# A 47-point Fourier stage moved from one 94x96 weight to four 47x64 weights in the quarters of the array

## The chip, the cores and the metric

The kernel runs on one core of one Trainium2 chip. The metric is the time of one execution on the device in microseconds (us); of several executions the median is taken. Below, PE is the matrix engine (TensorE), PEld its weight loads, ACT the ScalarE, DVE the VectorE, POOL the GpSimd engine, and SP the engine that issues most of the DMAs.

## What is computed

The reference has two parts, one behind the other. The first is a filter over the sequence, done in frequency space; the second is a two-layer network with a PReLU between its layers.

```python
X = np.fft.rfft(x, axis=1)                 # x: 8 batches, 3008 positions, 256 channels
Y = X * (filt_r + 1j * filt_i)[None]       # 1505 frequencies
y = np.fft.irfft(Y, n=3008, axis=1)
h = y.reshape(24064, 256) @ w_in           # 256 -> 2048
g = np.maximum(h, 0) + alpha * np.minimum(h, 0)
out = g @ w_out                            # 2048 -> 256
```

## The kernel before, in words

3008 is 47 times 64, so the transform of one batch is made in two stages. Stage a takes, for each of the 64 values of the position modulo 64 (called s) and for each of the 256 channels, a 47-point transform; only 24 of its 47 frequencies are needed, and their real and imaginary parts make 48 rows. Stage b makes the 64-point transforms with the twiddle factors in the weights, then the filter is applied, and stages c and d go back the same way. The result lies in `yT`, from which the network reads blocks of 512 positions.

The two parts run interleaved. The network has 47 blocks, each of 16 steps, so there are 752 steps, a little over 1 us each. In every step PE makes, in this order: the pieces of the transform that the plan puts at this step (`plan`, filled by `put`), the first layer of one slice of 128 hidden units (`up`, L616, two matmuls of 512 columns into `hps`), and a share of the second layer of an earlier block (L667, L689). The plan is fixed: the table `PLACES` holds, for each of batches 1 to 7, the step of every piece, and the same loops add the DMAs. Batch 0 has its own code (class `First`) and runs before the network starts. Engines take their instructions in the order in which the code issues them.

The pieces touched by the change are those of stage a of batches 1 to 7:

- `load_x` (L197) brings 8 values of s for each half (h = 0 is s below 32, h = 1 the rest) of one batch into a tile `xs`. Half 0 lies on partitions 0 to 46, half 1 on 47 to 93, with 8 x 256 values in each partition. Four such chunks c make a batch, with two DMAs on POOL's queue each (L201).
- `piece_a` (L237) multiplies the 94x96 weight `wf1_s`, which has the 47x48 matrix twice on its diagonal, with 512 columns of `xs` (L245), into one PSUM bank, and copies 96x512 values from there to `asb` on ACT (`on_act`, L324). 16 pieces make a batch, four a chunk.
- `save_a` (L249) writes the 96 partitions of `asb` to `a_dram` with one DMA from SP's queue (L250), once per chunk. When all four are written, `turn_a` (L252) reads them back in another order into `at` (L257), which stage b multiplies (`piece_b`, L261, matmuls at L265, copied by ACT at L269).

All pieces of stages a to d take their PSUM bank from `bank()` (L218): two pools `psF` of one bank each, used in turn. Whoever takes a bank waits until the copy out of its last user is done; so a user waits for the user two before it. The first layer has two tiles `hps` of its own, and ACT copies these too (L632).

In the setup, `turn_i` (L487) makes matmuls with weights of 64 columns, whose results go to PSUM partitions 0 to 63 and 64 to 127 in turn; line L502 has one matmul with 16 rows. Everything else uses the array as one tile of 128x128.

Of the kernel before, what the change touches and what calls it, by code (L numbers as in the profile page):

```python
# [10 lines left out]
FP16 = mybir.dt.float16  # L11
# [3 lines left out]
N1 = 47  # L15
N2 = 64
NK1 = 24
D = 256
# [60 lines left out]
def _build_consts():  # L79

    s1 = np.arange(N1)
    s2 = np.arange(N2)
    k1 = np.arange(NK1)
    p = np.arange(64)
    k2 = np.where(p < 32, p, 95 - p)
    g = np.where(p < 32, 1.0, -1.0)  # L90

    a1 = 2 * np.pi * np.outer(s1, k1) / N1
    wf1 = np.zeros((2 * N1, 96))
    wi3 = np.zeros((96, 2 * N1))
    scale = np.where(k1 == 0, 1.0, 2.0) / NFFT
    for h in range(2):
        r = slice(h * N1, h * N1 + N1)
        wf1[r, h * 48 : h * 48 + NK1] = np.cos(a1)
        wf1[r, h * 48 + NK1 : h * 48 + 48] = -np.sin(a1)
        wi3[h * NK1 : h * NK1 + NK1, r] = (np.cos(a1) * scale).T  # L100
        wi3[48 + h * NK1 : 48 + h * NK1 + NK1, r] = (-np.sin(a1) * scale).T

    kk = k1[:, None] + 47 * k2[None, :]
    ang = 2 * np.pi * s2[:, None, None] * kk[None, :, :] / NFFT
    c, s = np.cos(ang), np.sin(ang)
    twf = np.empty((128, NK1, 128))
    twf[:64, :, 64:], twf[64:, :, 64:] = c, s
    twf[:64, :, :64], twf[64:, :, :64] = -s * g, c * g
    return wf1, wi3, twf
# [3 lines left out]
def kernel(  # L113
# [9 lines left out]
):  # L123
    nc = tc.nc
    wf1_np, wi3_np, twf_np = _build_consts()
    wf1_d = nc.inline_tensor(wf1_np.astype(np.float16), name="c_wf1")
    wi3_np = wi3_np.reshape(4, NK1, 2 * N1).transpose(1, 0, 2).reshape(96, 2 * N1)
    wi3_d = nc.inline_tensor(wi3_np.astype(np.float16), name="c_wi3")
    wiz_np = np.zeros((3, 32, 4, 4, 2 * N1))
# [17 lines left out]
    konst = ctx.enter_context(tc.tile_pool(name="konst", bufs=1))  # L147
    p_x = ctx.enter_context(tc.tile_pool(name="p_x", bufs=4))
    p_fft = ctx.enter_context(tc.tile_pool(name="p_fft", bufs=1))
    p_as = ctx.enter_context(tc.tile_pool(name="p_as", bufs=2))  # L150
# [6 lines left out]
    a_dram = dram.tile([NB, 96, NH, D], FP16, name="a_dram")  # L157
# [1 line left out]
    ctx.enter_context(tc.manual_schedule())  # L159


    wf1_s = konst.tile([2 * N1, 96], FP16, name="wf1_s")
    wi3_s = konst.tile([96, 2 * N1], FP16, name="wi3_s")
    twf_s = konst.tile([128, NK1, 128], FP16, name="twf_s")
    twi_s = konst.tile([128, NK1, 128], FP16, name="twi_s")
# [18 lines left out]
    id16, wfx_s = idx_s[:, 0:128], idx_s[0 : 2 * N1, 128:224]  # L184
# [8 lines left out]
    def xrow(b, h, c):  # L193
        return bass.AP(tensor=x.tensor, offset=x.offset + (b * NFFT + NH * h + 8 * c) * D,
                       ap=[[N2 * D, N1], [1, 8 * D]])

    def load_x(b, c, halves=(0, 1)):  # L197
        if 0 in halves:
            xc[(b, c)] = p_x.tile([2 * N1, 8 * D], FP16, name="xs")
        for h in halves:  # L200
            nc.gpsimd.dma_start(out=xc[(b, c)][h * N1 : h * N1 + N1], in_=xrow(b, h, c))  # L201

    def load_filt(dst, pbase, src, ka, kb):
        n = kb - ka
# [13 lines left out]
    def bank(wide=False):  # L218
        if wide:
            return psH.tile([128, 2, 512], FP32, name="hps")[:, 0]  # L220
        turns[0] += 1
        return psF[turns[0] % 2].tile([128, 512], FP32, name="psF")
# [8 lines left out]
    class Fft:  # L231
# [2 lines left out]
            self.base = (b % 2) * NFFT  # L234
            self.uw, self.zt, self.asb = {}, {}, {}

        def piece_a(self, i, evict, wide=False):  # L237
            if i == 0:
                self.at = p_fft.tile([128, NK1, D], FP16, name="at")
            if i % 4 == 0:  # L240
                self.asb[i // 4] = p_as.tile([96, 8, D], FP16, name="asb")
            xs = xc[(self.b, i // 4)]
            ps = bank(wide)
            o = (i % 4) * 512
            nc.tensor.matmul(ps[0:96], wf1_s, xs[:, o : o + 512], start=True, stop=True)  # L245
            u = 2 * (i % 4)
            evict(self.asb[i // 4][:, u : u + 2].rearrange("p a d -> p (a d)"), ps[0:96])

        def save_a(self, c):  # L249
            nc.sync.dma_start(out=a_dram[self.b, :, 8 * c : 8 * c + 8], in_=self.asb[c])  # L250

        def turn_a(self, eng, ka=0, kb=NK1):  # L252
            for h in range(2):
# [78 lines left out]
    class First(Fft):  # L332
# [8 lines left out]
        def piece_a(self, i, evict, ps):  # L341
            c, sh, f = i // 4, (i // 2) % 2, i % 2
            for u in range(4):
                o = (4 * sh + u) * D + 128 * f
                nc.tensor.matmul(ps[:, 96 * u : 96 * u + 96], xc[(0, c)][:, o : o + 128], wfx_s,
                                 start=True, stop=True)
            s0 = 8 * c + 4 * sh
            evict(self.am.rearrange("p (f m s) -> p f m s", f=2, s=NH)[:, f, :, s0 : s0 + 4],
                  ps[:, 0:384].rearrange("p (s m) -> p m s", s=4))
# [78 lines left out]
    xc = {}  # L428
# [12 lines left out]
    for c in range(4):  # L441
        load_x(0, c)
# [120 lines left out]
    for c in range(4):  # L563
        load_x(1, c)
        if c == 0:
            load_w(1)
    for q in range(2):
        nc.gpsimd.dma_start(
            out=wout_s[:, 8 * q : 8 * q + 8],
            in_=moe_w_out[1024 * q : 1024 * q + 1024].rearrange("(j p) d -> p j d", p=128))  # L570
# [175 lines left out]
    def put(step, fn, *args):  # L746
        plan.setdefault(step, []).append((fn, args))
# [17 lines left out]
    for b in range(1, NB):  # L765
        p = 94 * (b - 1)
        f = Fft(b)
        steps_a, steps_b, steps_c, steps_d = PLACES[b - 1]
        for i in range(16):
            put(p + steps_a[i], f.piece_a, i, on_act)  # L770
            if i % 4 == 3:
                put(p + steps_a[i] + (b > 2), f.save_a, i // 4)
        if b + 1 < NB:
            for c in range(4):
                if b < 3:
                    put(LOADS[b - 1][c], load_x, b + 1, c)
                else:
                    for h in range(2):
                        put(p + LOADS[b - 1][2 * c + h], load_x, b + 1, c, (h,))
        quarters, later = (4, 1) if b < 3 else (1, 4)  # L780
        w = NK1 // quarters
        for q in range(quarters):
            put(p + steps_a[15] + (7 if b == 4 else later), f.turn_a, nc.sync, w * q, w * q + w)
        for kp in range(12):
            put(p + steps_b[kp], f.piece_b, kp)
            put(p + steps_c[kp], f.piece_c, kp, on_act)
            if kp % 3 == 2:
                put(p + steps_c[kp] + 1, f.turn_c, kp // 3)
        for i in range(16):
            put(p + steps_d[i], f.piece_d, i, on_act)  # L790
        put(p + steps_d[3] + 2, f.load_z, 3)
# [91 lines left out]
```

## Time and profile before

| what | us |
|---|---|
| median of 3 timed runs | 764.0 (763.15 to 765.53) |
| the profiled execution | 761.9 |
| its span, first to last instruction | 760.1 |
| PE busy in the span | 743.8 (98%) |
| DVE busy | 694.1 (91%) |
| ACT busy | 673.8 (89%) |
| stage a of batches 1 to 7: matmuls at L245 | 112 instructions, 35.7 to 549.6 |

The profile is one execution, recorded instruction by instruction. A row of a group names line, engine, operation, output and input tile, partitions x elements, and the count; then the busy time in us, the mean of one in ns, and the time for which the engine stood idle just ahead of these instructions, with what ended that. A row of the timeline begins with a start in us from the span's start and a length; "x7" says that seven instructions follow each other there, and the length reaches from the first one's start to the last one's end. The lengths of matmuls hold the passage through the array, so that consecutive matmuls overlap in the record: what a matmul costs PE is the distance from its start to the next one's.

### The profile page before, as it was taken

The page shows a single profiled execution, that of the slowest core. Times are in us where ns is not written, and L with a number is a line of the kernel's source. Part 1 is how long each engine was busy: PE and PEld are TensorE (multiplying, and loading weights), DVE is VectorE, ACT ScalarE, POOL GpSimd, SP SyncE. Part 2 cuts the span into 40 slices and gives each one's busy share as a digit, 9 for nine tenths or more (in the row PEclk, how much of TensorE's full clock was granted, in tenths as well). Part 3 has the DMA queues.
Part 4 walks back from the last instruction along what each step waited for, and adds up shares of the span by engine and source line. Part 5 has one row for each costly group of instructions (what it writes and reads, how often), then busy time and mean ns, then how long its engine had stood idle before and what let it go on. Part 6 is the DMA issues. An engine that isn't in the chain of part 4 may idle for free.

```text
span 760.1 us, 19854 instructions
## 1 busy us (share of the span) xinstructions
PE 743.8 (98%) x7812; PEld 539.9 (71%) x7812; DVE 694.1 (91%) x1298; ACT 673.8 (89%) x1083; POOL 163.8 (22%) x236
## 2 busy tenths in 40 slices
PE   6999999999999999999999999999999999999998
PEld 5756666776787777777778777777777777777766
DVE  5787887998999998899999999999998997999994
ACT  6898999999999988999899998999989898888873
POOL 8631421232022210232022211221100221010100
PEclk9999999999999999999999999999999999999999
DMA  9995888877965596766876659865486355522122
GB/s 160 196 236 152 148 182 214 174 149 170 211 150 114 120 192 160 148 121 140 189 161 143 136 117 197 187 141 113 106 185 135 77 105 113 138 63 66 43 65 62
DMA packets 100790, 107.97 MB, mean 142 GB/s; under 512 B 10568, under 2 KB 81496, under 8 KB 100696
## 3 DMA queue, kind: packets, MB, share of 16 engines
q1 hardware_dynamic: 80136, 70.05, 36.0%
q0 software_dynamic: 20416, 36.58, 29.8%
q8 instruction: 61, 1.00, 0.6%
q14 instruction: 33, 0.27, 0.1%
q10 hardware_dynamic: 144, 0.07, 0.0%
HBM read 55.41 MB, written 46.66 MB: 134 GB/s over the span
## 4 chain that ended last, share of the span: by engine, by line
PE 88%; DMA 5%; ACT 3%; POOL 2%; issue 1%; DVE 1%; DVEq 0%; POOLq 0%; ACTq 0%
PE hps L616 40%; PE op L689 30%; PE op L667 7%; PE psF L245 3%; PE psF L317 3%; PE psF L265 2%; PE psF L292 2%; DMA uw_s<-uw_s 2%; ACT gtb L632 2%; DMA xs<-in_x_dram 1%; DMA win_s<-in_moe_w_in_dram 1%; DMA filt<-in_filt_r_dram 1%; PE op L721 1%; ACT v L324 1%; POOL xs L201 1%
## 5 line engine op out<-in xcount | busy, mean ns | idle before, releaser
L616 PE MATMUL hps<-yT,win_s 128*128 128x512 f16 (+3 forms) x1600 | 447.4, 366 | 0.4 <-POOL win_s L575 0.4
L632 ACT ACTIVATE gtb<-hps 128x1024 f16<-128x1024 f32 x376 | 385.9, 1028 | 50.4 <-PE hps L616 47.5
L689 PEld LDWEIGHTS <-gtb 128*128 128x128 f16 x3040 | 206.0, 98 | 99.5 <-issue 0.3
L638 DVE TENSOR_SCALAR m_s<-gtb,alm_s 128x512 f16<-128x512 f16 x705 | 213.9, 347 | 38.4 <-ACT gtb L632 36.7
L819 DVE TENSOR_TENSOR gtb<-gtb,m_s 128x2048 f16<-128x2048 f16 x188 | 228.8, 1217 | 5.7 <-ACT m_s L636 3.2
L689 PE MATMUL op<-wout_s,gtb 128*128 128x128 f16 x1824 | 153.3, 219 | 0.0
L616 PEld LDWEIGHTS <-win_s 128*128 128x128 f16 x1600 | 135.4, 98 | 24.8 <-issue 2.9
L281 POOL DMA_DIRECT2D uw_s<-uw_s x84 | 72.3, 1003 | 330.0 <-DVE uw_s L278 205.7
L689 PEld LDWEIGHTS <-ss 128*128 128x128 f16 x1216 | 83.1, 98 | 37.4
L689 PE MATMUL op<-tw_s,gtb 128*128 128x128 f16 x1216 | 105.0, 219 | 0.0
L689 PE MATMUL op<-tw_s,ss 128*128 128x128 f16 x1216 | 103.4, 219 | 0.0
L667 PE MATMUL op<-wout_s,gtb 128*128 128x256 f16 x512 | 76.9, 273 | 0.3 <-DVE osb L592 0.3
L654 POOL DMA_DIRECT2D gtb<-gtb x28 | 28.5, 1017 | 208.0 <-ACT gtb L632 139.5
L667 PEld LDWEIGHTS <-gtb 128*128 128x128 f16 x512 | 49.9, 98 | 31.3
L324 ACT ACTIVATE asb<-psF 96x512 f16<-96x512 f32 x112 | 65.6, 601 | 1.8 <-PE psF L245 0.9
L324 ACT ACTIVATE yT<-psF 128x376 f16<-128x376 f32 x118 | 56.8, 493 | 4.7 <-PE psF L317 3.7
L324 ACT ACTIVATE v<-psF 128x512 f16<-128x512 f32 x88 | 52.1, 604 | 5.2 <-PE psF L292 4.0
L278 DVE TENSOR_TENSOR uw_s<-uw_s,filt 128x2048 f16<-128x2048 f16 x42 | 51.1, 1217 | 2.6 <-DMA uw_s<-uw_s 2.1
L201 POOL DMA_DIRECT2D xs<-in_x_dram x64 | 52.4, 986 | 5.1 <-issue 2.4
L269 ACT ACTIVATE uw_s<-psF 128x512 f16<-128x512 f32 x84 | 50.1, 605 | 3.0 <-PE psF L265 2.1
L650 DVE TENSOR_TENSOR ss<-ss,gtb 128x1024 f16<-128x1024 f16 x76 | 51.8, 682 | 0.1
L648 DVE TENSOR_TENSOR ss<-gtb 128x1024 f16<-128x1024 f16 (+1 forms) x75 | 51.7, 689 | 0.0
(125 smaller groups left out, 644.3 us busy)
## 6 DMA issues: line engine op xcount, KB each, us to landing
out_dram<-osb SPq DMA_DIRECT2D x127, 128.0 KB
xs<-in_x_dram POOLq DMA_DIRECT2D x64, 188.0 KB, 5.7
a_dram<-asb SPq DMA_DIRECT2D x28, 384.0 KB
uw_s<-uw_s POOLq DMA_DIRECT2D x84, 128.0 KB, 3.4
v_dram<-v SPq DMA_DIRECT2D x112, 96.0 KB
zt<-v_dram SPq DMA_DIRECT2D x28, 384.0 KB
at<-a_dram SPq DMA_DIRECT2D x20, 384.0 KB
gtb<-gtb POOLq DMA_DIRECT2D x28, 256.0 KB, 4.0
```

The source lines that it names most:

```text
L201: nc.gpsimd.dma_start(out=xc[(b, c)][h * N1 : h * N1 + N1], in_=xrow(b, h, c))
L278: nc.vector.tensor_mul(w.rearrange("p (i d) -> p i d", d=1024)[:, 0 : iu // 2 + 1 : iu // 2], uu.unsqueeze(1).to_broadcast([128, 2, 1024]), f)
L281: nc.gpsimd.dma_start(out=uu[o : o + 64], in_=ww[64 - o : 128 - o], accum_op=OP.add)
L324: nc.scalar.activation(o, i, AF.Copy)
L616: nc.tensor.matmul(self.hps[:, j % 2, ca:cb], win_s[:, kt, j * 128 : (j + 1) * 128], yT[:, kt, at : at + cb - ca], start=(kt == 0), stop=( ...
L632: nc.scalar.activation(g, hs, AF.Copy)
L638: nc.vector.tensor_scalar(ms[:, i], g[:, i], 0.0, a, OP.min, OP.mult)
L648: nc.vector.tensor_add(z1, a21, a22)
L650: nc.vector.tensor_add(z2, z1, a11)
L667: nc.tensor.matmul(op[:, si % 2], self.pair(k // 2)[:, k % 2, 128 * si : 128 * si + 128], wout_s[:, k], start=(k == 0), stop=(k == 15))
L689: nc.tensor.matmul(acc[:, 128 * i : 128 * i + 128], x[:, k, 128 * i : 128 * i + 128], b[:, k], start=first and k + i == 0, stop=k == 7, sk ...
L819: nc.vector.tensor_add(g, g, ms)
```

## The change

Stage a of batches 1 to 7 uses the array as four tiles of 64x64. The weight is a 128x64 tile that holds the 47x48 matrix, with 16 columns of zeros, on partitions 0 to 46 and again on 64 to 110. `load_x` puts half 1 of `x` on partition 64 instead of 47 (for batch 0 it stays at 47). A piece takes 512 columns of each half at two places (u = 0, 1), four matmuls, one in each quarter: half 0 writes one PSUM bank, half 1 the other, u chooses the partitions 0 to 63 or 64 to 127. So a piece takes two banks, and 8 pieces make a batch in place of 16. There are still 16 copies per batch, now of 128x512. The new piece i stands at the step of the old piece 2i + 1, and `save_a` at the same step as before, now as two DMAs of 48 partitions each.

```diff
+    wfq_np = np.zeros((2, 64, 64))
+    wfq_np[:, 0:N1, 0:48] = wf1_np[0:N1, 0:48]
...
-    wf1_s = konst.tile([2 * N1, 96], FP16, name="wf1_s")
+    wf1_s = konst.tile([128, 64], FP16, name="wf1_s")
...
         for h in halves:
-            nc.gpsimd.dma_start(out=xc[(b, c)][h * N1 : h * N1 + N1], in_=xrow(b, h, c))
+            o = h * (64 if b else N1)
+            nc.gpsimd.dma_start(out=xc[(b, c)][o : o + N1], in_=xrow(b, h, c))
...
-        def piece_a(self, i, evict, wide=False):
+        def piece_a(self, i, evict):
+            c, j = i // 2, i % 2
...
-            ps = bank(wide)
-            o = (i % 4) * 512
-            nc.tensor.matmul(ps[0:96], wf1_s, xs[:, o : o + 512], start=True, stop=True)
-            u = 2 * (i % 4)
-            evict(self.asb[i // 4][:, u : u + 2].rearrange("p a d -> p (a d)"), ps[0:96])
+            ps = (bank(), bank())
+            for u in range(2):
+                for h in range(2):
+                    r = slice(64 * h, 64 * h + N1)
+                    o = 1024 * u + 512 * j
+                    nc.tensor.matmul(ps[h][64 * u : 64 * u + 64], wf1_s[r], xc[(self.b, c)][r, o : o + 512],
+                                     start=True, stop=True)
+            for h in range(2):
+                evict(self.asb[c][:, h, 2 * j : 2 * j + 2].rearrange("p a d -> p (a d)"), ps[h])
 
         def save_a(self, c):
-            nc.sync.dma_start(out=a_dram[self.b, :, 8 * c : 8 * c + 8], in_=self.asb[c])
+            for u in range(2):
+                s = 8 * c + 4 * u
+                nc.sync.dma_start(out=a_dram[self.b, :, s : s + 4].rearrange("(h m) s d -> m h s d", h=2),
+                                  in_=self.asb[c][64 * u : 64 * u + 48])
...
-        for i in range(16):
-            put(p + steps_a[i], f.piece_a, i, on_act)
-            if i % 4 == 3:
-                put(p + steps_a[i] + (b > 2), f.save_a, i // 4)
+        for i in range(8):
+            put(p + steps_a[2 * i + 1], f.piece_a, i, on_act)
+            if i % 2:
+                put(p + steps_a[2 * i + 1] + (b > 2), f.save_a, i // 2)
```

More of the change, by code (lines that the diff above doesn't have):

```diff
@@ L125 @@
     wf1_np, wi3_np, twf_np = _build_consts()
-    wf1_d = nc.inline_tensor(wf1_np.astype(np.float16), name="c_wf1")
+    wfq_np = np.zeros((2, 64, 64))
+    wfq_np[:, 0:N1, 0:48] = wf1_np[0:N1, 0:48]
+    wf1_d = nc.inline_tensor(wfq_np.reshape(128, 64).astype(np.float16), name="c_wf1")
     wi3_np = wi3_np.reshape(4, NK1, 2 * N1).transpose(1, 0, 2).reshape(96, 2 * N1)
@@ L198, in load_x @@
         if 0 in halves:
-            xc[(b, c)] = p_x.tile([2 * N1, 8 * D], FP16, name="xs")
+            xc[(b, c)] = p_x.tile([128, 8 * D], FP16, name="xs")
         for h in halves:
-            nc.gpsimd.dma_start(out=xc[(b, c)][h * N1 : h * N1 + N1], in_=xrow(b, h, c))
+            o = h * (64 if b else N1)
+            nc.gpsimd.dma_start(out=xc[(b, c)][o : o + N1], in_=xrow(b, h, c))
     def load_filt(dst, pbase, src, ka, kb):
@@ L235, in __init__ @@
             self.uw, self.zt, self.asb = {}, {}, {}
-        def piece_a(self, i, evict, wide=False):
+        def piece_a(self, i, evict):
+            c, j = i // 2, i % 2
             if i == 0:
                 self.at = p_fft.tile([128, NK1, D], FP16, name="at")
-            if i % 4 == 0:
-                self.asb[i // 4] = p_as.tile([96, 8, D], FP16, name="asb")
-            xs = xc[(self.b, i // 4)]
-            ps = bank(wide)
-            o = (i % 4) * 512
-            nc.tensor.matmul(ps[0:96], wf1_s, xs[:, o : o + 512], start=True, stop=True)
-            u = 2 * (i % 4)
-            evict(self.asb[i // 4][:, u : u + 2].rearrange("p a d -> p (a d)"), ps[0:96])
+            if j == 0:
+                self.asb[c] = p_as.tile([128, 2, 4, D], FP16, name="asb")
+            ps = (bank(), bank())
[7 more added lines that the diff above has]
+                evict(self.asb[c][:, h, 2 * j : 2 * j + 2].rearrange("p a d -> p (a d)"), ps[h])
         def save_a(self, c):
-            nc.sync.dma_start(out=a_dram[self.b, :, 8 * c : 8 * c + 8], in_=self.asb[c])
+            for u in range(2):
+                s = 8 * c + 4 * u
+                nc.sync.dma_start(out=a_dram[self.b, :, s : s + 4].rearrange("(h m) s d -> m h s d", h=2),
+                                  in_=self.asb[c][64 * u : 64 * u + 48])
         def turn_a(self, eng, ka=0, kb=NK1):
@@ L344, in piece_a @@
                 o = (4 * sh + u) * D + 128 * f
-                nc.tensor.matmul(ps[:, 96 * u : 96 * u + 96], xc[(0, c)][:, o : o + 128], wfx_s,
+                nc.tensor.matmul(ps[:, 96 * u : 96 * u + 96], xc[(0, c)][0 : 2 * N1, o : o + 128], wfx_s,
                                  start=True, stop=True)
```

## The prediction

> **What bounds the kernel now.** I read the page first: the busy shares, the granted clock, and the chain that ended last.
>
> ```profile
> span 760.1 us, 19854 instructions
> ...
> PE 743.8 (98%) x7812; PEld 539.9 (71%) x7812; DVE 694.1 (91%) x1298; ACT 673.8 (89%) x1083; POOL 163.8 (22%) x236
> ...
> PEclk9999999999999999999999999999999999999999
> ...
> PE 88%; DMA 5%; ACT 3%; POOL 2%; issue 1%; DVE 1%; DVEq 0%; POOLq 0%; ACTq 0%
> ```
>
> PE is busy for 98% of the span, with its granted clock in the top step in every slice, and makes 88% of the chain. But a busy PE need not be full, so the next view is that of the groups of PE, by form.
>
> ```profile
> L616 PE MATMUL hps<-yT,win_s 128*128 128x512 f16 x1408 | 418.6, 379 | 0.4 <-POOL win_s L575 0.4
> ...
> L245 PE MATMUL psF<-xs,wf_s 94*96 94x512 f16 x112 | 41.7, 381 | 1.8 <-ACT asb L324 0.8 <-DVE zt L327 0.5 <-DVE yT L327 0.2
> L317 PE MATMUL psF<-wi_s,zt 96*128 96x94 f16 x496 | 40.3, 204 | 1.4 <-ACT yT L324 1.0 <-ACT asb L324 0.3
> L265 PE MATMUL psF<-at,twf_s 128*128 128x256 f16 x168 | 31.1, 272 | 0.2 <-DMA v_dram<-v 0.2
> ...
> L345 PE MATMUL op<-idx_s,xs 94*128 94x96 f16 x32 | 2.7, 206 | 0.3 <-DVE gtb L327 0.3
> ...
> L487 PE MATMUL hps<-idx_s,ss 128*64 128x128 f16 x32 | 1.3, 222 | 0.0
> ```
>
> The idle times are small: 0.4 us before all of L616, 1.8 us before all of L245. So PE does run one matmul behind the other, and what a matmul costs is the distance to the next start. The timeline of PE around the first pieces shows it.
>
> ```profile
> 35.28 0.60 PE L616 MATMUL hps<-yT,win_s 128*128 128x512 f16 x2
> 35.71 0.38 PE L245 MATMUL psF<-xs,wf_s 94*96 94x512 f16 x1
> 35.93 0.38 PE L616 MATMUL hps<-yT,win_s 128*128 128x512 f16 x1
> ```
>
> Two full-array matmuls of 512 columns take 35.28 to 35.71, about 0.216 each; the piece with its 96-column weight takes 0.22. All 112 pieces cost 112 x 0.22 = 24.6 us of PE, two of them 0.44. A microsecond saved or lost on PE is one on the clock.
>
> **Part 1: the matmuls.** 112 matmuls go, and 56 groups of four quarter matmuls come. If the four stream side by side, a group takes one pass of 512 columns, 0.216. Does the trace show such a thing? Once, in the setup: L487 uses the array as two halves of 64 columns.
>
> ```profile
> 9.07 0.34 PE L345 MATMUL op<-idx_s,xs 94*128 94x96 f16 x4
> 9.34 0.25 PE L487 MATMUL hps<-idx_s,ss 128*64 128x128 f16 x2
> ...
> 9.34 0.64 PE L487 MATMUL hps<-idx_s,ss 128*64 128x128 f16 x16
> ...
> 9.91 0.22 PE L345 MATMUL psF<-idx_s,xs 94*128 94x96 f16 x1
> ...
> 544.82 0.55 PE L689 MATMUL op<-tw_s,ss 128*128 128x128 f16 x7
> ```
>
> Sixteen half matmuls of 128 columns take 0.64, the last of them 0.22, so 0.42 for fifteen steps; that is about 0.055 a pair. Full-array matmuls of 128 columns take (0.55 - 0.22) / 6 = 0.055 each. So the two halves do stream together, and the second member of a pair costs some 0.003.
>
> The edges of this stretch are what decides. Going in: the four at L345 begin at 9.07 and end at 9.41, so the last (206 ns) began at 9.20; their spacing is 0.13 / 3 = 0.043, so the next could begin at 9.247. It began at 9.34: **0.093 late**, and its first two last 0.25 where the mean is 0.222: another 0.024. Going out: the last half matmul began at 9.34 + 0.64 - 0.22 = 9.76, the next could begin at 9.81 and began at 9.91: **0.10 late**. A change of the array's division costs about 0.1 us each way.
>
> In the network's stretch each group stands alone between full-array matmuls (plan, then `up` and the second layer in every step), so it pays both edges: 0.093 + 0.024 + 0.216 + 3 x 0.003 + 0.10 = 0.44 us, against 0.44 for the two old pieces. The sum is 56 x 0.44 = 24.7 us: **+0.1**. The halved streaming is spent on the edges. Bounds: with free edges a group costs 0.226, 56 x 0.214 = 12.0 us gained; if the two row halves stream one after the other, 56 x 0.216 = 12.1 lost. I take 0.44, because both edges were seen and no row shows them free. That row halves run together no row of before shows; L487 divides columns only, and it is the nearest row.
>
> [...]
>
> **Part 2: two banks at once.** A piece took one bank and waited for the user two before it. A group takes both: its first matmul needs the older bank, its second the one that the user directly before it has just filled. In the changed program 48 of the 56 second matmuls wait for ACT. So the question is how long a copy takes to finish, and how close the user before stands. In the trace of before this wait occurs already where a piece follows two others closely:
>
> ```profile
> 110.31 1.06 ACT L324 ACTIVATE v<-psF 128x512 f16<-128x512 f32 x2
> ...
> 110.99 0.82 PE L245 MATMUL psF<-xs,wf_s 94*96 94x512 f16 x2
> ```
>
> The second piece began at 110.99 + 0.82 - 0.38 = 111.43, just behind the copy's end at 111.37, where it could have begun at 111.21.
>
> For each of the 56 groups I took its place from the trace (the start of the second old piece of its pair, or of the first where both stand together) and the end of the copy of the `psF` user before it. The wait is the difference less the 0.12 of the edge, which passes meanwhile. 25 groups wait, 14.8 us in all. The first, the longest and the last:
>
> ```profile
> 38.28 0.49 ACT L324 ACTIVATE yT<-psF 128x376 f16<-128x376 f32 x1
> ...
> 38.36 0.38 PE L245 MATMUL psF<-xs,wf_s 94*96 94x512 f16 x1 [0.50 <-DVE zt L327]
> ...
> 154.45 0.38 PE L265 MATMUL psF<-at,twf_s 128*128 128x256 f16 x2
> 154.67 0.38 PE L245 MATMUL psF<-xs,wf_s 94*96 94x512 f16 x1
> ...
> 154.32 1.01 ACT L632 ACTIVATE gtb<-hps 128x1024 f16<-128x1024 f32 x1
> 155.22 0.38 ACT L716 ACTIVATE osb<-op 128x256 f32<-128x256 f32 x1
> 155.49 0.60 ACT L269 ACTIVATE uw_s<-psF 128x512 f16<-128x512 f32 x1
> ...
> 545.21 0.38 PE L292 MATMUL psF<-uw_s,twi_s 128*128 128x256 f16 x2
> 545.43 0.38 PE L245 MATMUL psF<-xs,wf_s 94*96 94x512 f16 x1
> ...
> 545.63 0.60 ACT L324 ACTIVATE v<-psF 128x512 f16<-128x512 f32 x1
> ```
>
> At 154.67 the old piece went on at once, into the other bank. The new group would need the bank that L265 filled at 154.45, whose copy ACT begins at 155.49, behind a copy of `hps` and one of the output, and ends at 156.09: a wait of 1.42 - 0.12 = 1.30. At 38.36 it is 38.77 - 38.36 - 0.12 = 0.29, at 545.43 it is 546.23 - 545.43 - 0.12 = 0.68. Eleven groups stand 0.22 or less behind another user in the same step and carry 10.3 of the 14.8. Behind a waiting group stand `up` and the second layer of its step on PE, and ACT waits for their `hps`; nothing makes that up, since PE is full.
>
> The lower bound: if ACT were always free, a copy would begin as the matmuls end, and of the pair at 154.45 it would end at 154.83 + 0.04 + 0.605 = 155.48 (the 0.04 is 545.63 less 545.21 + 0.38), a wait of 0.69; the same working over the 25 gives 7.7. I take 14.8, because ACT's order keeps the copies ahead where they are. Behind the groups, the next users wait for two copies made one after the other: up to 3.8 us over 16 places by the same working; I take 2. The idle time of 1.8 before L245 goes.
>
> **Part 3: the copies, the moves, the DMAs.** The copies are 16 per batch as before.
>
> ```profile
> L324 ACT ACTIVATE asb<-psF 96x512 f16<-96x512 f32 x112 | 65.6, 601 | 1.8 <-PE psF L245 0.9
> ...
> L324 ACT ACTIVATE v<-psF 128x512 f16<-128x512 f32 x87 | 51.8, 606 | 5.2 <-PE psF L292 4.0 <-PE psF L390 0.5
> ```
>
> 128 partitions take 606 ns where 96 take 601: 112 x 0.005 = 0.6 us of ACT, which hides in its 11% of idle time. POOL issues the same DMAs for `x`. The 28 saves become 56, with parts of 2 KB where they had 4 KB.
>
> ```profile
> L250 SPq DMA_DIRECT2D a_dram<-asb x28: 303/324/962, 42.0 to 553.7; - x28
> ...
> SPq L257 <- DMA a_dram<-asb: 9.7, 4, 3.9
> ```
>
> SP spends 28 x 0.324 = 9.1 us more, and the stores queued behind move by that much each time. Only the last save of a batch is on a path: L257 waits for it, and L265 for L257; L265 waited 0.2 us for DMAs in the whole run (row above). I cost it at nothing, hidden by the steps between L257 and L265; without that cover, each batch would lose the extra issue and one copy, 7 x 0.93 = 6.5 us.
>
> **The sum.** 0.1 + 14.8 + 2.0 - 1.8 = +15.1 us: a span of 775.2. Around it lie 1.8 us (761.9 less 760.1), so the run profiled would take 777.0. The median, 764.0, stood 2.1 above that run; so I predict 779.
>
> **The rivals.** *Row halves in turn* (0.11): the change does not do what it says, the two row halves don't stream together. For it: no row shows row halves. Against: L487's column halves do. 779 + 12 = 791. *Free edges* (0.09): a group costs 0.226, 12.0 us less; the waits lose the cover of the edge, 25 x 0.12 = 3.0 more. 764.0 - 12.0 + 14.8 + 3.0 + 2.0 - 1.8 = 770. For it: the rows of L487 carry no group of 512 columns; against: two edges with 0.1 each. *Faster than before* (0.04): free edges at both ends of the group, 12.0 us on PE. It decides as soon as the waits come to less than that; at their lower end (7.7, with eleven lost covers of 0.12) the time is 764.0 - 12.0 + 7.7 + 1.3 - 1.8 = 759. *The way through DRAM* (0.03): stage b begins late in every batch, 779 + 6.5 = 785.
>
> **How the numbers follow.** My forecast has 0.73, with 770 (0.1 + 7.7 - 1.8, the waits' lower bound) to 785 as its own range. The range of 768 to 790 leaves out row halves in turn, faster than before, and some 0.05 of tails: 0.20. A measurement tells 0.3% from no change, 761.7 to 766.3. Faster by more: 0.04; within: 0.03, from the low tail of the free edges; slower: 0.93.
>
> **What would show it.** In the changed profile the four matmuls of a group start within 0.01 us of each other where they don't wait (right), or 0.216 apart by rows (rival). From the end of the last full-array pass to the next full-array start it is 0.44 for a group that does not wait; 0.23 means free edges. The idle time ahead of the stage-a matmuls grows from 1.8 to about 15 us, ended by ACT's copies of `uw_s`, `v` and `yT`. If that idle time stays under 5 us, part 2 is wrong; if L265 waits for DMAs for more than 2 us, part 3 is.

## The result and the profile after

The changed kernel takes 785.12 us (median of 4, 783.96 to 789.11), the kernel before 764.76 (median of 4): the ratio is 1.0276, with a 95% interval of 1.0232 to 1.0320. So it is slower, by some 20 us; 15 were forecast. The profiled execution took 785.8, its span 784.0.

The page of the changed kernel, beside that of before: the span, the busy times, the chain. Stage a is now at L251, and the lines behind it stand ten further down (L265 is L275, L616 is L626).

```profile
span 784.0 us, 20101 instructions
...
PE 756.6 (97%) x7924; PEld 537.6 (69%) x7924; DVE 695.9 (89%) x1298; ACT 678.7 (87%) x1083; POOL 163.1 (21%) x236
...
PE 76%; DMA 9%; ACT 9%; issue 2%; DVE 2%; POOL 1%; SPq 0%; DVEq 0%; ACTq 0%; POOLq 0%
```

PE fell from 88% of the chain to 76%, ACT rose from 3% to 9% and the DMAs from 5% to 9%: the work that ends last now runs through waits. The groups of PE by form say where they stand:

```profile
L327 PE MATMUL psF<-wi_s,zt 96*128 96x94 f16 x496 | 40.3, 204 | 2.3 <-DMA zt<-v_dram 1.4 <-ACT yT L334 0.8
L251 PE MATMUL psF<-xs,wf_s 47*64 47x512 f16 x224 | 32.4, 396 | 8.9 <-ACT uw_s L279 4.1 <-ACT v L334 2.0 <-DVE zt L337 1.3
L275 PE MATMUL psF<-at,twf_s 128*128 128x256 f16 x168 | 31.1, 272 | 0.5 <-ACT uw_s L279 0.3
L302 PE MATMUL psF<-uw_s,twi_s 128*128 128x256 f16 x168 | 31.0, 272 | 3.8 <-DMA uw_s<-uw_s 3.2 <-ACT asb L334 0.6
```

The idle time ahead of stage a went from 1.8 to 8.9 us, ended by the copies of `uw_s` and `v`, as forecast. It is less than the forecast 15 because the column counts only time in which nothing runs: the first quarter matmul of a group covers the beginning of the wait (at the place with the longest wait worked out, below, the column has 0.83 of 1.23). The starts tell more. A group that does not wait, in the timeline of PE:

```profile
54.47 0.60 PE L677 MATMUL op<-wout_s,gtb 128*128 128x256 f16 x4
55.00 0.41 PE L251 MATMUL psF<-xs,wf_s 47*64 47x512 f16 x4
55.34 0.61 PE L626 MATMUL hps<-yT,win_s 128*128 128x512 f16 x2
```

Four matmuls with rows on both halves last 0.41 in all, where one lasts 0.40: all four quarters stream together, 0.003 apart by their starts. The pass before ends at 54.91 (54.47 + 0.60 - 0.27 is the last start, and 256 columns take 0.109, the distance of the starts of two such matmuls), so the group begins 0.09 late; 55.34 is 0.33 behind the last quarter's start, 0.216 of pass and 0.116 of edge. From 54.91 to 55.34 it is 0.43.

The place that the prediction took as its longest example, in the timelines of PE and of ACT:

```profile
160.94 0.38 PE L275 MATMUL psF<-at,twf_s 128*128 128x256 f16 x2
161.25 0.40 PE L251 MATMUL psF<-xs,wf_s 47*64 47x512 f16 x1
162.48 0.41 PE L251 MATMUL psF<-xs,wf_s 47*64 47x512 f16 x3 [0.83 <-ACT uw_s L279]
162.82 0.39 PE L626 MATMUL hps<-yT,win_s 128*128 128x512 f16 x1
...
160.64 1.03 ACT L642 ACTIVATE gtb<-hps 128x1024 f16<-128x1024 f32 x1
161.56 0.38 ACT L726 ACTIVATE osb<-op 128x256 f32<-128x256 f32 x1
161.82 0.60 ACT L279 ACTIVATE uw_s<-psF 128x512 f16<-128x512 f32 x1
```

The first quarter goes, the second waits for the bank that L275 filled, until ACT is through at 162.42: 162.48 - 161.25 = 1.23 where 1.30 was worked out.

Over the 56 groups, from the end of the pass before to the start of the next full-array matmul, the instruction records give 42.9 us. A group without a wait takes 0.436 (the middle one of 26 such), 24.4 for all; so 18.5 us are waits, 16.6 of them inside the group and 1.9 ahead of its first matmul. The 112 old pieces took 24.6 and waited 3.2 by the same measure. That is +15.1 of the 23.9 us by which the span grew. Ahead of the users behind (L302, L327, L275, L434) the gaps grew by 4.5 us, ahead of the second layer by 2.1, and the pass behind each group takes 0.226 in place of 0.216, 0.6 in all. Another 1.7 came from a thing that no row of before showed. The windows of PE around 125 us, with the granted clock in the column behind POOL's:

```profile
118.80:122.20 3.40, 3.18 (x36) 1.96 (x33) 2.49 (x6) 3.40 (x7) 0.00 (x0) 1.00 0.47 136
122.20:125.64 3.44, 1.65 (x22) 1.25 (x23) 2.76 (x5) 2.45 (x6) 0.00 (x0) 1.00 0.99 270
125.64:129.05 3.41, 3.41 (x20) 2.10 (x18) 1.79 (x4) 1.66 (x3) 0.94 (x1) 0.50 1.07 369
129.05:132.50 3.45, 3.45 (x35) 1.99 (x34) 1.39 (x5) 2.50 (x5) 0.00 (x0) 1.00 0.65 142
```

PE was busy for 1.65 of 3.44 us and stood waiting for most of the rest (one wait for `zt` took 1.37), and then ran at half clock for 3.41 us. In this stretch seven matmuls of 128 columns at L699 took 0.75 us from the first start to the next group's (125.86 to 126.61), where seven of them took 0.39 at full clock (120.60 to 120.99). The 1.7 is half of 3.41, an estimate.

### The profile page after: what moved, and what is told of

Its sections match the earlier page's. It is cut to its first block, busy times and chain, and to the rows that moved or that the text cites. A ratio compares the mean times of both kernels' runs of the same rounds, so it can differ in the third digit from the quotient of the medians.

```text
span 784.0 us, 20101 instructions
## 1 busy us (share of the span) xinstructions
PE 756.6 (97%) x7924; PEld 537.6 (69%) x7924; DVE 695.9 (89%) x1298; ACT 678.7 (87%) x1083; POOL 163.1 (21%) x236
## 4 chain that ended last, share of the span: by engine, by line
PE 76%; DMA 9%; ACT 9%; issue 2%; DVE 2%; POOL 1%; SPq 0%; DVEq 0%; ACTq 0%; POOLq 0%
PE hps L626 34%; PE op L699 26%; PE op L677 5%; DMA uw_s<-uw_s 3%; ACT gtb L642 3%; PE psF L251 2%; PE psF L327 2%; PE psF L302 2%; PE psF L275 2%; DMA win_s<-in_moe_w_in_dram 1%; DMA xs<-in_x_dram 1%; ACT asb L334 1%; DMA at<-a_dram 1%; ACT uw_s L279 1%; DMA filt<-filt 1%
## 5 line engine op out<-in xcount | busy, mean ns | idle before, releaser
L626 PE MATMUL hps<-yT,win_s 128*128 128x512 f16 (+3 forms) x1600 | 448.6, 367 | 0.0
L699 PEld LDWEIGHTS <-gtb 128*128 128x128 f16 x3040 | 207.0, 98 | 100.5 <-issue 2.1
L699 PE MATMUL op<-wout_s,gtb 128*128 128x128 f16 x1824 | 153.3, 219 | 0.1
L626 PEld LDWEIGHTS <-win_s 128*128 128x128 f16 x1600 | 129.6, 98 | 22.7 <-issue 13.5
L699 PEld LDWEIGHTS <-ss 128*128 128x128 f16 x1216 | 83.2, 98 | 37.8 <-DVE ss L660 0.3
L699 PE MATMUL op<-tw_s,gtb 128*128 128x128 f16 x1216 | 105.9, 220 | 0.0
L699 PE MATMUL op<-tw_s,ss 128*128 128x128 f16 x1216 | 103.8, 219 | 0.1
L334 ACT ACTIVATE asb<-psF 128x512 f16<-128x512 f32 x112 | 61.0, 601 | 14.1 <-PE psF L251 14.0
```

What stands on the lines that cost most here:

```text
L334: nc.scalar.activation(o, i, AF.Copy)
L626: nc.tensor.matmul(self.hps[:, j % 2, ca:cb], win_s[:, kt, j * 128 : (j + 1) * 128], yT[:, kt, at : at + cb - ca], start=(kt == 0), stop=( ...
L699: nc.tensor.matmul(acc[:, 128 * i : 128 * i + 128], x[:, k, 128 * i : 128 * i + 128], b[:, k], start=first and k + i == 0, stop=k == 7, sk ...
```

## The experiments

The theory: PE gains nothing by the quarters, since the two edges of a group eat what the shared pass saves; the loss is the wait for the second bank. The rivals: the edges are the loss and the waits would be there anyway; the saves as two DMAs are the loss.

**The waits without quarters.** The kernel before, its full-array pieces at the places of the groups:

```diff
-            put(p + steps_a[i], f.piece_a, i, on_act)
+            put(p + steps_a[i | 1], f.piece_a, i, on_act)
```

> The kernel before with its full-array pieces taken two at a time, at the step of the second one, as the changed kernel takes its groups; no quarter of the array is used. Theory (a group's matmuls cost what two old pieces cost, the loss is the wait for two PSUM banks at one place): the time is near that of the changed kernel, 778 to 786, with 12 to 20 us of waits ahead of the stage-a matmuls. Rival (the edges of the division into quarters are the loss): 763 to 767.

Measured: 778.59 us, ratio 1.0185 (1.0156 to 1.0214) against the 763.76 of before on that chip, +14.8 (here and below the difference in us is that of the medians). The group of stage a, and one place in the timeline:

```profile
L245 PE MATMUL psF<-xs,wf_s 94*96 94x512 f16 x112 | 37.1, 379 | 10.9 <-ACT uw_s L269 4.8 <-ACT v L324 2.5 <-DVE zt L327 1.7
...
155.98 0.38 PE L265 MATMUL psF<-at,twf_s 128*128 128x256 f16 x2
156.19 0.38 PE L245 MATMUL psF<-xs,wf_s 94*96 94x512 f16 x1
157.52 0.38 PE L245 MATMUL psF<-xs,wf_s 94*96 94x512 f16 x1 [0.94 <-ACT uw_s L269]
```

No quarter is used, and the same waits are there at the same places, with the same releasers: the second piece stands 1.33 behind the first where 0.22 would do. The bank and the place make them, not the division of the array. Over the 56 places they come to 15.1 us by the starts, against 18.5 in the changed kernel.

**The edges without waits.** The kernel before with one small quarter matmul ahead of every second piece:

```diff
+            if i % 2:
+                nc.tensor.matmul(ps[0:64, 0:16], wf1_s[0:N1, 0:64], xs[0:N1, o : o + 16], start=True, stop=True)
             nc.tensor.matmul(ps[0:96], wf1_s, xs[:, o : o + 512], start=True, stop=True)
```

> The kernel before with one extra matmul of 16 columns on a 64x64 quarter, ahead of each second piece and into its bank, which that piece then overwrites: 56 times the edges, no bank taken earlier. Theory (an edge costs 0.093 going in and 0.116 going out, whatever stands around it): 56 x 0.22 = 12.3 us, so 776 to 779. Rival (in the network's stretch an edge is mostly hidden by other waits): under 770.

Measured: 777.16, ratio 1.0167 (1.0139 to 1.0195), +13.4 us, or 0.24 for each of the 56. By the starts: 0.093 going in, 0.123 from the small matmul to the piece, and 0.033 more on the piece itself, 0.25 together.

```profile
L247 PE MATMUL psF<-xs,wf_s 94*96 94x512 f16 x112 | 44.4, 399 | 0.3 <-ACT asb L326 0.3
L246 PE MATMUL psF<-xs,wf_s 47*64 47x16 f16 x56 | 10.7, 192 | 1.0 <-DVE zt L329 0.7 <-DVE yT L329 0.2
```

The idle column shows next to nothing: an edge is no idle time of this view, since the records of the passes before and behind reach over it. Only the distance of starts shows it. The edges are real in the network's stretch, and worth about what the shared pass saves (12.0).

**Both kinds of division.** The same, in turn by rows alone and by columns alone:

```diff
+            if i % 4 == 1:
+                nc.tensor.matmul(ps[0:96, 0:16], wf1_s[0:N1], xs[0:N1, o : o + 16], start=True, stop=True)
+            if i % 4 == 3:
+                nc.tensor.matmul(ps[0:48, 0:16], wf1_s[:, 0:48], xs[:, o : o + 16], start=True, stop=True)
             nc.tensor.matmul(ps[0:96], wf1_s, xs[:, o : o + 512], start=True, stop=True)
```

> The kernel before with one extra matmul of 16 columns ahead of each second piece, in turn as a half of the array by rows (47 rows, 96 columns) and as a half by columns (94 rows, 48 columns); the piece then overwrites it. [...] Rival (only a division by columns, or only one by rows, costs the edge): one kind shows under 0.02 going in.

Measured, in one run: 775.59, against 764.23 for the kernel before. One place of each kind, in the timeline of PE:

```profile
99.70 0.60 PE L671 MATMUL op<-wout_s,gtb 128*128 128x256 f16 x4
100.23 0.21 PE L246 MATMUL psF<-xs,wf_s 47*96 47x16 f16 x1
100.37 0.42 PE L249 MATMUL psF<-xs,wf_s 94*96 94x512 f16 x1
...
103.45 0.60 PE L671 MATMUL op<-wout_s,gtb 128*128 128x256 f16 x4
103.98 0.19 PE L248 MATMUL psF<-xs,wf_s 94*48 94x16 f16 x1
104.10 0.42 PE L249 MATMUL psF<-xs,wf_s 94*96 94x512 f16 x1
```

Both small matmuls start 0.53 behind the start of four matmuls of 256 columns that need 0.44: 0.09 going in, either way, so the rival falls. Going out it is 0.14 behind the start of the one by rows, a little above the 0.123 of the small quarter matmul, and 0.12 behind the one by columns.

**Groups of one bank.** One half of `x`, two quarters side by side, at the 16 old steps:

```diff
-            ps = (bank(), bank())
-            for u in range(2):
-                for h in range(2):
...
+            ps = bank()
+            for u in range(2):
+                r = slice(64 * h, 64 * h + N1)
...
+            evict(self.asb[c][:, h, 2 * j : 2 * j + 2].rearrange("p a d -> p (a d)"), ps)
```

> The changed kernel with groups of one bank: each takes one half of x, two quarters side by side (u = 0 and 1), one pass of 512 columns and one copy, 16 groups per batch at the steps of the 16 old pieces. No group needs two banks at once, but there are 112 pairs of edges and no streaming is saved. Theory (edges add at every group, 0.093 + 0.116 + 0.010 each): 112 x 0.22 = 24.5 us over before, less what hides behind the few waits, 785 to 790, with under 5 us of waits at the groups. Rival (the two-bank wait is the whole loss): under 772.

Measured: 785.59, ratio 1.0292 (1.0254 to 1.0331), +21.4 us. The group row of stage a reads:

```profile
L250 PE MATMUL psF<-xs,wf_s 47*64 47x512 f16 x224 | 42.5, 399 | 2.0 <-DVE zt L335 1.0 <-ACT asb L332 0.8
```

The idle time is back at 2.0, as before the change: one bank, no such wait. Nearly twice the edges (at nine places two groups follow each other directly and share them) and hardly a saved pass cost about the same as one set of edges, a saved pass and the waits. So the rival that the bank is all of it falls as well: the gain is lost to the edges, the loss comes from the bank.

**The saves.** The kernel before with its saves split:

```diff
-            nc.sync.dma_start(out=a_dram[self.b, :, 8 * c : 8 * c + 8], in_=self.asb[c])
+            for u in range(2):
+                s = 8 * c + 4 * u
+                nc.sync.dma_start(out=a_dram[self.b, :, s : s + 4], in_=self.asb[c][:, 4 * u : 4 * u + 4])
```

> The kernel before with each save of stage a as two DMAs with parts of 2 KB in place of one with parts of 4 KB, issued at the same step. Theory (the saves are covered): within 1 us of before, 763 to 766. Rival (the extra issues and shorter parts make stage b or the reading of v late): 767 to 771.

Measured: 764.15 against 764.23, ratio 0.9995 (0.9976 to 1.0013). The saves cost nothing; this rival falls.

**Groups moved apart.** The changed kernel with a place for each group that is chosen by how many other users of `psF` stand near (`busy` counts them by step):

```diff
+                def price(s):
+                    return (10 * busy.get(s, 0) + 4 * busy.get(s - 1, 0) + 2 * busy.get(s - 2, 0)
+                            + 3 * busy.get(s + 1, 0) + 0.1 * abs(s - p - steps_a[2 * i + 1]))
+                s = min(range(lo, hi + 1), key=price)
...
-            put(p + steps_a[2 * i + 1], f.piece_a, i, on_act)
+            put(where[b, i], f.piece_a, i, on_act)
```

> The changed kernel with each of its 56 groups moved by a few steps (from the step of the first old piece of its pair to four steps behind the second), to where the fewest other users of the psF banks stand in the same step, the two before and the one behind. Theory (the waits for a copy just ahead are the loss): the 18.5 us of waits at the groups fall to under 8, the time to 768 to 775. Rival (the loss sits in the division itself, or in the saves as two DMAs): 780 to 786.

Measured: 788.30, ratio 1.0310 (1.0284 to 1.0336), +24.5, which is above the theory and the rival alike. The waits at the groups fell only to 15.2 us (39.6 less 24.4). Against the starts of the first layer in the kernel before, this run had lost 15.1 us when that one stood at 161 us, and only another 10.3 behind it; for the changed kernel it is 8.1 and 15.5. Summed over the groups, the waits of batches 1 and 2 rose from 5.1 to 9.2 us, those of batches 3 to 7 fell from 13.4 to 6.0. Three windows of 3.41 us ran at half clock, all in the first part (some 5 us lost, if each costs half of itself). So the places were kept for batches 1 and 2 and moved for 3 to 7:

```diff
+                if b < 3:
+                    lo = hi = p + steps_a[2 * i + 1]
```

> The spread groups for batches 3 to 7 alone; batches 1 and 2 stay at the steps of the changed kernel. In the first spread run the delay against before grew by 15.1 us up to 161 us of the old time, where it grew by 8.1 in the changed kernel, and behind that by 10.3, where it grew by 15.5. Theory (spreading helps where there is room and does harm where the steps are dense): 8.1 + 10.3 = 18.4 less the half-clock windows, 779 to 783. Rival (the places make no difference, the sum only moves about): 785 to 789.

Measured: 777.70, ratio 1.0176 (1.0145 to 1.0207), +13.5, so some 7 us better than the changed kernel and better than expected. Its group row:

```profile
L252 PE MATMUL psF<-xs,wf_s 47*64 47x512 f16 x224 | 29.3, 397 | 4.4 <-ACT v L335 1.4 <-DVE zt L338 1.4 <-ACT asb L335 0.8
```

8.9 has become 4.4, and the waits by the starts are 35.4 less 24.4, 11.0 us (5.0 in batches 1 and 2, 6.0 in the others). Where the schedule has room, other places take more than half of the wait away. There is little to win behind that: with no wait left, 56 groups cost 24.4 us and the pass behind each 0.6 more, where the old pieces without their 3.2 us of waits cost 24.6.

**The halves outermost.** Both matmuls of half 0 first, so that the first bank is complete while the second waits:

```diff
-            for u in range(2):
-                for h in range(2):
+            for h in range(2):
+                for u in range(2):
```

> The changed kernel with the two matmuls of half 0 first and the two of half 1 behind them, so that the first bank is complete, and its copy can run, while the second waits. Theory: the waits ahead of the second bank stay as they are, but the users behind wait less: 1 to 4 us gained, 781 to 784. Rival (row halves no longer overlap, since the wait stands between them): a waiting group costs a pass of 0.216 more, 25 x 0.2 = 5 us lost, 790.

Measured: 785.37, ratio 1.0274 (1.0240 to 1.0307): no gain and no loss that can be told; the 1 to 4 us expected did not come. Against the rival, a waiting group did not cost a pass more: the group row of stage a has 32.0 us busy behind 9.0 idle, where the changed kernel's has 32.4 behind 8.9. Whether the earlier copy helped anybody stays open, for the clock covers it: the profiled run had four windows at half clock, the changed kernel's had one. With half of each window taken off as lost, which is an estimate, its span is 779.5 us against 782.3. These rows are those around the last window:

```profile
292.70:296.10 3.40, 3.34 (x37) 2.24 (x34) 3.40 (x9) 2.81 (x4) 0.00 (x0) 1.00 1.20 222
296.10:299.50 3.40, 1.18 (x12) 0.90 (x13) 2.72 (x4) 0.75 (x2) 0.00 (x0) 1.00 0.83 235
299.50:302.90 3.40, 3.40 (x21) 2.14 (x19) 2.60 (x3) 2.72 (x4) 0.00 (x0) 0.50 0.02 6
```

## Why the prediction was right

The sign, the mechanism and the range of 768 to 790 held; the sum was 6 us short of the measured median (779 against 785.1), which lies 0.1 above the forecast's own range of 770 to 785.

- **Part 1, the matmuls: right.** 0.44 was forecast for a group, 0.436 measured. The terms moved a little: going out took 0.116 in place of 0.10, and the 0.024 of the first matmul did not appear inside the group but as 0.010 on the next pass. All four quarters ran together, 0.003 apart, so the rival of row halves in turn falls, and so does that of free edges, with 0.093 measured going in and 0.116 going out. What PE does in this time no run shows.
- **Part 2, two banks at once: the mechanism right, the term too small.** 14.8 us were worked out for the wait at the second bank, and 16.6 were measured inside the groups. The lower bound of 7.7 was far off: ACT's order did keep the copies where they were. Of the 1.8 us that were missing, 0.9 fall to batch 1, where 1.2 were forecast and 2.1 came. These places were priced by the trace of before, one by one; where groups follow each other closely, each is shifted by the last one's wait and copies, and the price taken from the old places no longer holds. The other 1.9 of the 18.5 us stand ahead of the first matmul of two groups, the first and the last of batch 1:

```profile
38.59 0.59 PE L251 MATMUL psF<-xs,wf_s 47*64 47x512 f16 x4 [1.13 <-DVE zt L337]
...
59.24 0.89 PE L251 MATMUL psF<-xs,wf_s 47*64 47x512 f16 x4 [0.67 <-ACT asb L334]
```

Old pieces had waited at both places too, 0.66 and 0.77 by the starts. The prediction let all old waits go (the -1.8 of its sum), and these stayed. They were also mis-sized: 3.2 by the starts, where the idle column showed 1.8. The users behind lost about 4.5 us and the second layer 2.1, where 2 had been taken for all, and most of the users' wait was another one than forecast. It was to be the wait for two copies made one after the other; in the rows above, the idle time ahead of L302 and L327 that is new ends mostly with DMAs (`uw_s` 3.2, `zt` 1.4). Before, the row of L302 read as below, and that of L317 named no DMA. Why these land later was not traced.

```profile
L292 PE MATMUL psF<-uw_s,twi_s 128*128 128x256 f16 x168 | 31.1, 273 | 2.0 <-DMA uw_s<-uw_s 1.0 <-ACT gtb L632 1.0
```

- **Part 3, copies and saves: right.** The copies take 601 ns for 128 partitions, as for 96, and the split saves measured nothing. The rival of the way through DRAM had named 785, the time that came, but not its cause: L275 stood idle for 0.5 us in all. What ACT lost is the time in which it waits for a group (the row of the copies in the changed kernel; 1.8 before):

```profile
L334 ACT ACTIVATE asb<-psF 128x512 f16<-128x512 f32 x112 | 61.0, 601 | 14.1 <-PE psF L251 14.0
```

- **What was missing:** the half clock, 1.7 us in the profiled run by the estimate above. Of the changed kernel's four runs two had a mean clock of 1.000 (783.96 and 784.44), the others 0.998 (785.80) and 0.993 (789.11).
- **What stays open:** the waits alone (+14.8) and the edges alone (+13.4) less the saved passes (12.0) make +16.2, some 4 us less than the changed kernel. Part of that rest can be read from the starts of the two profiles. At almost every place that waits, the wait is 0.12 longer in the changed kernel than in the run without quarters, and over all places it is 18.5 against 15.1 us. In the run without quarters the first piece makes its pass of 0.216 inside the wait; of a group, only the edge going in (0.093) falls into it. So the saved passes are worth less than 12.0 where groups wait. The half clock may be another part (1.7 in the profile of the changed kernel, none in the profiles of those two runs). What then remains was not traced further.

## What to carry to other kernels

In this kernel, dividing the matrix engine cost 0.093 us going in and 0.116 going out, 0.21 together, about one pass of 512 columns (0.216): by this sum, an estimate, it would pay only where several divided passes follow each other without a full-array matmul in between, which no run here tried. Before two pieces are merged into one, look at what each of them waits for: with the pair of banks taken in turn the 112 old pieces waited 3.2 us in all, and the 56 groups that took both banks at once stood behind the copy of the last user, for 16.6 us. Price such a wait from the copies' ends in the trace, but price close neighbours together.

## What the runs showed of the hardware that was not expected

The granted clock of PE fell to 0.50 for 3.41 us at a time (once for two such stretches in a row), always directly behind a stretch of 3.41 us with little matmul work: in the windows read, PE was busy for 1.65 of 3.44 us in the changed kernel, for 1.41, 1.05 and 2.12 of 3.40 where the groups were moved apart, and for 1.78 of 3.42 and 1.18 of 3.40 with the halves outermost. With each pass counted from its start at 0.216 us for 512 columns, and passes that run side by side counted once, the stretches at full clock ahead of a fall had matmuls streaming for 0.26 to 0.42 of their length (eight, in the changed kernel, with 0.33, and three experiments); in these traces no stretch with 0.43 or more was followed by a fall, nor were two others with 0.42. In the profile of the kernel before, no stretch had less than 0.51, and the clock was 1.000 over the span; of its other executions some had a mean of 0.998. So on this kernel a wait of 1.4 us, with others beside it, cost up to 1.7 us more behind itself (half of 3.41, an estimate).
